# A chunked scan before two feed-forward blocks: how the first four chunks get their decay rows, and when

## The chip, the cores and the metric

The kernel runs on one core of one Trainium2 chip. The metric is the device time of one execution in microseconds, and the median of three runs is what counts. The core has five engines that run beside each other, each through its own list of instructions in order: PE (TensorE, matrix products), DVE (VectorE), ACT (ScalarE), POOL (GpSimd) and SP (SyncE, which here only issues transfers). Sixteen DMA engines carry the transfers, and an engine that has a transfer instruction in its list starts it and goes on.

## What is computed

A state-space scan over 4 batches, 8 heads, 768 steps, then a feed-forward block with an ELU, then a bilinear one. Cut to what matters here:

```python
def _attn_ref(x, a, B, C):                # x: 4 x 8 x 768 x 32, state width N = 16
    log_a = np.log(np.clip(a, 1e-06, 1.0))
    for c in range(nc):
        cum = np.cumsum(log_a[:, :, sl], axis=-1)
        L = np.exp(cum[..., :, None] - cum[..., None, :]) * causal
        M = np.einsum('bhin,bhjn->bhij', Cc, Bc) * L
        y[:, :, sl] = M @ xc + (Cc @ state) * np.exp(cum)[..., None]
        state = decay_full * state + (Bc * decay_from_j).T @ xc
...
h = x @ w_in                              # 3072 x 256 @ 256 x 2048
g = np.where(h > 0, h, np.exp(np.minimum(h, 0)) - 1)
x = g @ w_out                             # 2048 x 256
out = (((x @ w1) * (x @ w2)) @ w3) @ w_out2
```

`L` needs nothing but products of consecutive values of `a`. The kernel makes it by running products, without a logarithm.

## The kernel before

The scan works on 24 chunks of 128 steps, each as two halves of 64, with all eight heads at once. Four chunks make one tile of 512 tokens, and there are six tiles. All later products take every operand as a high and a low part in fp32r and use three matmuls for each (`mm3`). So each piece of a weight (512 KB) goes through three stages: a load (line 136), bit work on DVE and ACT (lines 146 to 148) and a split into the two parts (lines 103 and 104). The pieces of the first block are `wi0` to `wi7` (`raw_wi` in the profile) and `wo0` to `wo7` (`raw_wo`).

One chunk `k` of the first tile goes through four steps:

- `at_prep`: DVE makes `L` by one scan along the rows (line 334) from values of `a` that lie alike on all partitions of a half. POOL then makes `bd`, B times the decay to the chunk's end (line 340).
- `at_cb`: PE makes the products of C and B (`cb`, line 351), and DVE multiplies them into `L` (line 359).
- the state step: POOL makes `cd` from C and the running products `pr` (line 373), PE makes `u` (line 387), and DVE brings the state `st` forward (lines 396 and 399). `pr` is made once for four chunks by `at_decay` (lines 261 to 303).
- `at_y`: PE makes `y` from `L` and from the state (lines 416 and 422), ACT copies out its high part `xTh` (line 431), and DVE its low part `xTl` (line 432).

For chunks 4 and later the values of `a`, with 0 put at each half's first place, are written once to DRAM (`a_cut`), and each half of an `L` tile is filled from there by a transfer that gives the same 2 KB row to 64 partitions (line 312). For chunks 0 to 3 the values come another way. `at_first` loads all of `a` (`a_f`), bounds it, cuts it and splits it for PE. `at_wide` then has PE spread the rows over the partitions by products with a 0/1 matrix (`sel`; the result is `aw`, line 321).

The order of the first tile is a table, `ORDER`. A number is a step, 4k plus 0 for `at_prep`, 1 for `at_cb`, 2 for the state step and 3 for `at_y`. A pair is a weight piece and the stage to bring it to, `"pr"` is `at_decay(0)`, `"aw"` the second spreading product, and `"h"` the products of the first feed-forward unit for half of its tokens. After the table come the units of the feed-forward blocks, with the scan of later tiles laid between them. PSUM rooms for `cb`, `u`, `y` and `h` come from one pool of three that go round, so a `y` that isn't copied out holds back the third room request after it.

Every transfer reports its end on one of eight counters (`DMAHW0` to `DMAHW7`), handed out in turn as the transfers are scheduled, whatever engine issues them. Before a counter is used again, the issuing engine waits, in its own list, until the transfer that had it before has landed. Before the change only SP issues transfers.

Of the kernel before, what the change touches and what calls it, by code (L numbers as in the profile page):

```python
# [7 lines left out]
F32 = mybir.dt.float32  # L8
F32R = mybir.dt.float32r
# [4 lines left out]
NB, NH, S, D, N = 4, 8, 768, 32, 16  # L14
Q = 128
SUB = 2
R = Q // SUB
CPB = S // Q
NCHUNK = NB * CPB
TT = 512  # L20
NTILE = NB * S // TT
CPT = TT // Q
# [11 lines left out]
PACE, LATE, END, FIRST = 1.5, 12.0, 7.0, 8.0  # L34
SPILL, BACK = 3, 8

ORDER = [0, 4, 1, "pr", 2, "aw", (0, 2), 5, 3, 6, (0, 3), 8, 7, 9, (1, 2), 10, 12, 11, 13, (1, 3), 14, "h", 15, (2, 2), (3, 2)]


XCOLS = (("x", DM), ("bn", NH * N), ("bt", 2 * R), ("cz", 2 * 2 * R), ("cp", SUB * 2 * R))  # L40
# [3 lines left out]
def kernel(  # L44
# [20 lines left out]
    nc = tc.nc  # L65
    P = 128

    const = ctx.enter_context(tc.tile_pool(name="const", bufs=1))
    wts = ctx.enter_context(tc.tile_pool(name="wts", bufs=1))
    act = ctx.enter_context(tc.tile_pool(name="act", bufs=2))  # L70
    att = ctx.enter_context(tc.tile_pool(name="att", bufs=2))
    ps_w = ctx.enter_context(tc.tile_pool(name="ps_w", bufs=3, space=bass.MemoryType.PSUM))
    ps_a = ctx.enter_context(tc.tile_pool(name="ps_a", bufs=1, space=bass.MemoryType.PSUM))

    V, A, G, T = nc.vector, nc.scalar, nc.gpsimd, nc.tensor


    eye2 = const.tile([P, SUB, R], F32, name="eye2")
    eye = const.tile([P, NH, R], F32, name="eye")
    side = const.tile([P, 2], F32, name="side")  # L80
    sel = const.tile([SUB * CPT, CPT, SUB, R], F32R, name="sel")
    begun = const.tile([P, CPT * SUB, R], F32, name="begun")

    def constants():

        V.memset(side, 0.0)
        A.activation(side, side, AF.Exp)

        G.memset(eye2, 1.0)
        G.affine_select(out=eye2, in_=eye2, compare_op=ALU.is_equal, fill=0.0, base=0,  # L90
                        pattern=[[-R, SUB], [-1, R]], channel_multiplier=1)
        n = SUB * CPT
        A.copy(sel, eye2[:n, 0, :n].rearrange("p (k s o) -> p k s o", k=CPT, o=1).to_broadcast([n, CPT, SUB, R]))
        V.tensor_tensor(out=eye2[:, 0], in0=eye2[:, 0], in1=eye2[:, 1], op=ALU.add)
        V.tensor_copy(eye, eye2[:, 0:1].to_broadcast([P, NH, R]))
        G.memset(begun, 0.0)
# [69 lines left out]
    a = slice(None)  # L166
# [87 lines left out]
    ck = [{} for _ in range(NCHUNK)]  # L254
    xT = {}
    state = {}
    a_cut = tc.dram_tile([NCHUNK * SUB, NH, R], F32, name="a_cut")
    cut = []

    def clip(eng, out, v):  # L260
        return eng.tensor_scalar(out, v, 1e-6, 1.0, op0=ALU.max, op1=ALU.min)

    def at_first():


        t = act.tile([P, 2, NH, R], F32, tag="p", name="a_f")[:SUB * NCHUNK, 0]
        nc.sync.dma_start(t, a_s)
        clip(V, t, t)
        V.memset(t[:, :, 0:1], 0.0)
        n = SUB * CPT  # L270
        hl = act.tile([P, 2, NH, R], F32R, tag="p", name="a_hl")[:n]
        split(hl[:, 0], hl[:, 1], t[:n], V)
        cut.extend([hl, t])

    def at_load(k):
        c = ck[k]
        all_ = att.tile([P, XC], F32, tag="xbc", name=f"xbc{k}", bufs=4)
# [12 lines left out]

    def at_pr(t):

        pr[t] = att.tile([P, CPT * SUB, R], F32, tag="pr", name=f"pr{t}", bufs=2)
        nc.sync.dma_start(pr[t].rearrange("p k i -> p (k i)"),
                          a_h[t].rearrange("h (o s) -> h o s", o=1).to_broadcast([NH, N, TT]))

    def at_decay(t):

        v = pr[t]
        pace(clip(V, v, v))  # L300
        V.tensor_copy(begun[:, :, 0:1], v[:, :, 0:1])
        V.memset(v[:, :, 0:1], 0.0)  # L302
        V.tensor_tensor_scan(out=v.rearrange("p k i -> p (k i)"), data0=v.rearrange("p k i -> p (k i)"),
                             data1=begun.rearrange("p k i -> p (k i)"), initial=0.0, op0=ALU.mult, op1=ALU.add)

    def at_l(k):
        c = ck[k]
        c["L"] = att.tile([P, NH, R], F32, tag="L", name=f"L{k}", bufs=3)
        if k >= CPT:

            for s in range(SUB):
                nc.sync.dma_start(c["L"][R * s:R * s + R].rearrange("p h s -> p (h s)"),
                                  a_cut[SUB * k + s:SUB * k + s + 1].rearrange("s h i -> s (h i)").to_broadcast([R, NH * R]))

    def at_wide(k):


        wide = ps_a.tile([P, 2, TT], F32, tag="acc", name=f"aw{k}") if k else banks(f"aw{k}")
        for j in range(2):
            for p in range(2):  # L320
                mm = T.matmul(wide[:, j], sel[:, k + j].rearrange("r s i -> r (s i)"),
                              cut[0][:, p].rearrange("r h i -> r (h i)"), start=p == 0, stop=p == 1)
                if j == p == 0:
                    tc.keep_in_program_order(mm)
            ck[k + j]["a"] = wide[:, j]

    def at_prep(k):

        c = ck[k]
        L = c["L"]  # L330
        flat = wide = L.rearrange("p h s -> p (h s)")
        if k < CPT:
            wide = c["a"]
        made = V.tensor_tensor_scan(out=flat, data0=wide, data1=eye.rearrange("p h s -> p (h s)"), initial=0.0,
                                    op0=ALU.mult, op1=ALU.add)
        pace(made)
        if k < CPT:
            last_mm[:] = [made.ins]
        c["bd"] = att.tile([P, NH, N], F32, tag="bd", name=f"bd{k}")
        G.tensor_tensor(out=c["bd"], in0=c["bn"], in1=L[:, :, R - 1:R].to_broadcast([P, NH, N]), op=ALU.mult)  # L340

    def cb_products(k, cb):

        c = ck[k]
        for g in range(2):
            for r in range(4):
                s, b = divmod(r, 2)
                rows = slice(32 * r, 32 * r + 32)  # L350
                mm = T.matmul(cb[R * s:R * s + R, b, 2 * R * g:2 * R * g + 2 * R], c["bt"][rows, g], c["cz"][rows, g],  # L351
                              start=True, stop=True, skip_group_check=True)
                if k == g == r == 0:
                    tc.keep_in_program_order(mm)
        return mm

    def decayed(k, cb):
# [233 lines left out]
    made = 0  # L591
# [56 lines left out]
    queue, due = [], []  # L648
# [49 lines left out]

    at_first()
    constants()  # L700
    at_load(0)
    at_pr(0)
    queue[0].advance(1)
    for k in range(1, CPT):
        at_load(k)
    for p in queue[1:3]:
        p.advance(1)
    nc.sync.dma_start(a_cut, cut[1])
    for p in queue[3:8]:
        p.advance(1)  # L710
    for k in range(CPT):
        at_l(k)
    at_wide(0)
    for p in queue[:first_n]:
        p.lo = V

    for j in ORDER:
        if j == "pr":
            at_decay(0)
        elif j == "aw":  # L720
            at_wide(2)
# [82 lines left out]
```

## Time and profile before

| | us |
|---|---|
| median of 3 runs | 576.53 (576.19 to 577.77) |
| profiled execution, device time | 577.51 |
| its span in the trace | 575.8 |
| PE busy in the span | 553.8 (96%) |
| DVE busy | 338.4 (59%) |
| ACT busy | 273.3 (47%) |
| POOL busy | 85.8 (15%) |

The busy times are shares of the whole span, in which the stages differ much. The first 28 us hold the scan of the first tile, and up to about 60 us weight pieces are being made on DVE and ACT beside the first feed-forward units. After that PE is nearly always at work. In the rows below, us count from the span's start, and "issue" rows of SP show when SP issued a transfer, not when it landed.

### The profile page before, as it was taken

How to read it: one execution, taken by the hardware profiler on the slowest of the kernel's cores; microseconds unless marked ns; L12 is line 12 of the kernel's file. 1: busy time of each engine (PE TensorE's matmuls, PEld its weight loads, DVE VectorE, ACT ScalarE, POOL GpSimd, SP SyncE). 2: the span in 40 equal slices, each digit the busy share in tenths (PEclk: the TensorE clock that was granted, in tenths of full speed). 3: DMA queues.
4: the chain of work that ended last, by engine and by line, in shares of the span. 5: the costliest groups of instructions: out<-in, count | busy, mean ns of one | idle time of the engine just before them, and what ended most of it. 6: DMA issues, size and time to landing. Idle time of an engine off the chain costs nothing.

```text
span 575.8 us, 10500 instructions
## 1 busy us (share of the span) xinstructions
PE 553.8 (96%) x4436; PEld 442.1 (77%) x4436; DVE 338.4 (59%) x483; ACT 273.3 (47%) x375; POOL 85.8 (15%) x91
## 2 busy tenths in 40 slices
PE   5998998999999999999999999999999999999996
PEld 3675786788888888878787878877878868888784
DVE  6599999784976764756524444253766353244332
ACT  2296669445575565873214222222644452364222
POOL 2201324232204231550000000000111000000000
PEclk9998999899999999999999999999999999999999
DMA  8977453644333412550000421021000000000000
GB/s 289 332 235 235 135 163 121 201 155 150 114 139 131 135 70 102 190 146 1 0 1 37 157 83 56 0 94 56 37 19 2 1 2 0 1 37 0 1 1 36
DMA packets 27167, 52.78 MB, mean 92 GB/s; under 512 B 2192, under 2 KB 10384, under 8 KB 27120
## 3 DMA queue, kind: packets, MB, share of 16 engines
q1 hardware_dynamic: 27120, 52.11, 28.0%
q8 instruction: 35, 0.57, 0.5%
q14 instruction: 12, 0.10, 0.1%
HBM read 45.71 MB, written 6.39 MB: 90 GB/s over the span
## 4 chain that ended last, share of the span: by engine, by line
PE 79%; DVE 11%; issue 3%; ACT 3%; DMA 2%; POOL 1%; SPq 0%; DVEq 0%; POOLq 0%
PE ab L241 8%; PE ab L240 8%; PE ab L242 7%; PE acc_b L241 6%; PE acc_b L240 6%; PE acc_b L242 6%; PE h L240 6%; PE h L242 5%; PE h L241 5%; PE acc_d L241 4%; PE acc_d L240 4%; PE acc_d L242 4%; DMA raw_wa<-in_w 2%; PE s L351 2%; DVE e L523 1%
## 5 line engine op out<-in xcount | busy, mean ns | idle before, releaser
L523 DVE SCALAR_TENSOR_TENSOR e<-e,h 128x1024 f32<-128x1024 f32 x48 | 58.3, 1215 | 40.6 <-ACT e L522 40.5
L104 DVE TENSOR_TENSOR g<-e,g 128x1024 fp32r<-128x1024 f32 x48 | 60.2, 1255 | 34.9 <-ACT g L103 34.6
L240 PE MATMUL h<-xTh,w_in_lo 128*128 128x512 f32 (+1 forms) x196 | 77.5, 396 | 2.2 <-DVE pr L302 0.6
L240 PE MATMUL acc_b<-g,w_out_lo 128*128 128x512 f32 x192 | 77.1, 402 | 2.2 <-DVE x2l L104 1.9
L241 PE MATMUL acc_b<-g,w_out_hi 128*128 128x512 f32 x192 | 76.5, 399 | 1.0 <-DVE g L104 0.9
L103 ACT CAST g<-e 128x1024 fp32r<-128x1024 f32 x48 | 50.5, 1053 | 54.8 <-PE acc_b L242 30.2
L242 PE MATMUL acc_b<-g,w_out_hi 128*128 128x512 f32 x192 | 76.4, 398 | 0.0
L241 PE MATMUL h<-xTl,w_in_hi 128*128 128x512 f32 (+1 forms) x196 | 76.2, 389 | 0.0
L242 PE MATMUL h<-xTh,w_in_hi 128*128 128x512 f32 (+1 forms) x196 | 76.2, 389 | 0.0
L240 PE MATMUL ab<-x2h,w 128*128 128x512 f32 x192 | 74.2, 392 | 1.7 <-ACT x2h L103 1.4
L241 PE MATMUL ab<-x2l,w 128*128 128x512 f32 x192 | 75.0, 391 | 0.1
L242 PE MATMUL ab<-x2h,w 128*128 128x512 f32 x192 | 74.7, 389 | 0.0
L520 ACT ACTIVATE e<-h 128x1024 f32<-128x1024 f32 x48 | 49.3, 1028 | 42.5 <-PE h L242 39.9
L568 DVE TENSOR_TENSOR pa<-pa,ab 128x512 f32<-128x512 f32 x48 | 32.6, 685 | 59.1 <-ACT pa L567 59.1
L567 ACT COPY pa<-ab 128x512 f32<-128x512 f32 x48 | 27.9, 588 | 74.2 <-PE ab L242 73.6
L104 DVE TENSOR_TENSOR p<-pa,p 128x512 fp32r<-128x512 f32 x48 | 32.9, 690 | 40.4 <-ACT p L103 40.2
L103 ACT CAST p<-pa 128x512 fp32r<-128x512 f32 x48 | 29.8, 621 | 48.0 <-PE acc_d L242 28.6
L522 ACT ACTIVATE e<-e 128x1024 f32<-128x1024 f32 x48 | 51.2, 1066 | 0.9
L240 PEld LDWEIGHTS h<-xTh,w_in_lo 128*128 128x128 f32 x196 | 37.2, 190 | 11.3 <-DVE pr L302 0.9
L240 PEld LDWEIGHTS acc_b<-g,w_out_lo 128*128 128x128 f32 x192 | 36.6, 191 | 10.8 <-DVE x2l L104 2.1
L240 PEld LDWEIGHTS ab<-x2h,w 128*128 128x128 f32 x192 | 35.9, 188 | 10.6 <-ACT x2h L103 2.3
L241 PEld LDWEIGHTS acc_b<-g,w_out_hi 128*128 128x128 f32 x192 | 36.7, 191 | 9.1 <-DVE g L104 1.7
(106 smaller groups left out, 891.9 us busy)
## 6 DMA issues: line engine op xcount, KB each, us to landing
xbc<-in_xc SPq DMA_DIRECT2D x24, 512.0 KB, 6.0
raw_wc<-in_w3t SPq DMA_DIRECT2D x16, 512.0 KB, 3.4
L<-a_cut SPq DMA_DIRECT2D x40, 128.0 KB, 4.5
raw_wi<-in_w_in SPq DMA_DIRECT2D x8, 512.0 KB, 8.3
raw_wo<-in_w_out SPq DMA_DIRECT2D x8, 512.0 KB, 4.6
out_t<-o SPq DMA_DIRECT2D x12, 256.0 KB, 2.0
raw_wq<-in_wo SPq DMA_DIRECT2D x4, 512.0 KB, 3.4
raw_wb<-in_w SPq DMA_DIRECT2D x4, 512.0 KB, 6.1
```

The costliest lines, as they stand in the source:

```text
L103: A.copy(hi, raw)
L104: return lo_eng.tensor_tensor(out=lo, in0=raw, in1=hi.bitcast(F32), op=ALU.subtract)
L240: last_mm[:] = [T.matmul(out, wlo, xhi, start=first, stop=False, **kw).ins]
L241: T.matmul(out, whi, xlo, start=False, stop=False, **kw)
L242: T.matmul(out, whi, xhi, start=False, stop=last, **kw)
L351: mm = T.matmul(cb[R * s:R * s + R, b, 2 * R * g:2 * R * g + 2 * R], c["bt"][rows, g], c["cz"][rows, g], start=True, stop=True, skip_group ...
L520: A.activation(e, h, AF.Exp)
L522: A.activation(e, e, AF.Relu, scale=-1.0, bias=1.0)
L523: V.scalar_tensor_tensor(out=e, in0=e, scalar=-1.0, in1=h, op0=ALU.mult, op1=ALU.max)
L567: A.copy(e, h[:, 0])
L568: V.tensor_tensor(out=e, in0=e, in1=h[:, 1], op=ALU.mult)
```

## The change

- Chunks 0 and 1 (`DIRECT = 2`) get their `L` tiles by transfers straight from the input `a_s`, and DVE bounds and cuts each tile itself (`bounded`). Chunks 2 and 3 get theirs from `a_cut`, as later chunks do. The `L` tiles of the first tile are four rooms instead of three.
- The spreading products, `sel` and the split of `a` are gone.
- For chunks 0 to 3 the `L` transfers, and the one that writes `a_cut`, are issued by ACT instead of SP.
- `pr` is made behind the first `L`.
- The data of all four chunks are issued ahead of all weight pieces (before, the first piece stood ahead of chunk 1's data).
- The table has another order: the making of piece `wi0` stands later against the chunks, as does that of `wi1`.

```diff
-ORDER = [0, 4, 1, "pr", 2, "aw", (0, 2), 5, 3, 6, (0, 3), 8, 7, 9, (1, 2), 10, 12, 11, 13, (1, 3), 14, "h", 15, (2, 2), (3, 2)]
+DIRECT = 2
+
+ORDER = [0, "pr", 1, 2, 4, 5, 3, 6, (0, 2), 8, 7, 9, (0, 3), 10, 12, 11, 13, (1, 2), 14, "h", (1, 3), 15, (2, 2), (3, 2)]
...
         t = act.tile([P, 2, NH, R], F32, tag="p", name="a_f")[:SUB * NCHUNK, 0]
         nc.sync.dma_start(t, a_s)
-        clip(V, t, t)
-        V.memset(t[:, :, 0:1], 0.0)
-        n = SUB * CPT
-        hl = act.tile([P, 2, NH, R], F32R, tag="p", name="a_hl")[:n]
-        split(hl[:, 0], hl[:, 1], t[:n], V)
-        cut.extend([hl, t])
+        cut.append(t)
+
+    def bounded(v):
+        clip(V, v, v)
+        V.memset(v[:, :, 0:1], 0.0)
...
     def at_l(k):
+
         c = ck[k]
-        c["L"] = att.tile([P, NH, R], F32, tag="L", name=f"L{k}", bufs=3)
-        if k >= CPT:
-
-            for s in range(SUB):
-                nc.sync.dma_start(c["L"][R * s:R * s + R].rearrange("p h s -> p (h s)"),
-                                  a_cut[SUB * k + s:SUB * k + s + 1].rearrange("s h i -> s (h i)").to_broadcast([R, NH * R]))
...
+        c["L"] = att.tile([P, NH, R], F32, tag="L", name=f"L{k}", bufs=4)
+
+        for s in range(SUB):
+            (A if k < CPT else nc.sync).dma_start(
+                c["L"][R * s:R * s + R].rearrange("p h s -> p (h s)"),
+                (a_s if k < DIRECT else a_cut)[SUB * k + s:SUB * k + s + 1].rearrange("s h i -> s (h i)").to_broadcast([R, NH * R]))
...
-        flat = wide = L.rearrange("p h s -> p (h s)")
-        if k < CPT:
-            wide = c["a"]
-        made = V.tensor_tensor_scan(out=flat, data0=wide, data1=eye.rearrange("p h s -> p (h s)"), initial=0.0,
+        flat = L.rearrange("p h s -> p (h s)")
+        if k < DIRECT:
+            bounded(L)
+        made = V.tensor_tensor_scan(out=flat, data0=flat, data1=eye.rearrange("p h s -> p (h s)"), initial=0.0,
                                     op0=ALU.mult, op1=ALU.add)
...
+    for k in range(DIRECT):
+        at_l(k)
     at_first()
     constants()
     at_load(0)
     at_pr(0)
-    queue[0].advance(1)
     for k in range(1, CPT):
         at_load(k)
-    for p in queue[1:3]:
+    bounded(cut[0])
+    A.dma_start(a_cut, cut[0])
+    for k in range(DIRECT, CPT):
+        at_l(k)
+    for p in queue[:8]:
         p.advance(1)
-    nc.sync.dma_start(a_cut, cut[1])
-    for p in queue[3:8]:
-        p.advance(1)
-    for k in range(CPT):
-        at_l(k)
-    at_wide(0)
```

What this does to the lists of the engines shows best on ACT. Its list before, from the copy for the spreading products on; the number after a name's letters is the chunk or the piece (`raw_wi0`, `y1`), the last number only tells buffers apart, and the brackets name what the instruction waits for:

```order
L103 CAST a_hl_93<-a_f_89 8x512 [waits DVE_49]
L147 ACTIVATE raw_wi0_108<-raw_wi0_108 128x512 [waits DMAHW3_49]
L103 CAST w_in_hi_78<-raw_wi0_108 128x2x256 [waits DVE_49]
L431 CAST xTh0_218<-y0_193 128x2x2x64 [waits PE_49]
L431 CAST xTh0_218<-y1_244 128x2x2x64 [waits PE_49]
L147 ACTIVATE raw_wi1_116<-raw_wi1_116 128x512 [waits DMAHW7_49]
L103 CAST w_in_hi_78<-raw_wi1_116 128x2x256 [waits DVE_49]
L431 CAST xTh0_218<-y2_310 128x2x2x64 [waits PE_49]
L431 CAST xTh0_218<-y3_387 128x2x2x64 [waits PE_49]
```

And ACT's list after the change, from its fifth instruction on:

```order
L692 DMA a_cut_85<-a_f_94 48x512 [waits DMAHW1_49,DVE_49]
L309 DMA L2_116<-a_cut_85 64x512 [waits DMAHW1_49]
L309 DMA L2_116<-a_cut_85 64x512 [waits DMAHW3_49]
L309 DMA L3_119<-a_cut_85 64x512 [waits DMAHW5_49]
L309 DMA L3_119<-a_cut_85 64x512 [waits DMAHW7_49]
L415 CAST xTh0_212<-y0_187 128x2x2x64 [waits PE_49]
L146 ACTIVATE raw_wi0_122<-raw_wi0_122 128x512
L102 CAST w_in_hi_77<-raw_wi0_122 128x2x256 [waits DVE_49]
L415 CAST xTh0_212<-y1_237 128x2x2x64 [waits PE_49]
L415 CAST xTh0_212<-y2_304 128x2x2x64 [waits PE_49]
L146 ACTIVATE raw_wi1_124<-raw_wi1_124 128x512 [waits DMAHW4_49]
```

Five transfers, four of them with a wait on a landing counter, now stand on ACT ahead of the first copy out of a `y`. SP's list in the same program, from chunk 1's data on:

```order
L275 DMA xbc1_107<-in_xc 128x1024
L275 DMA xbc2_109<-in_xc 128x1024 [waits DMAHW0_49]
L275 DMA xbc3_111<-in_xc 128x1024 [waits DMAHW2_49]
L135 DMA raw_wi0_122<-in_w_in 128x2x512 [waits DMAHW3_49]
L135 DMA raw_wi1_124<-in_w_in 128x2x512 [waits DMAHW4_49]
L135 DMA raw_wi2_126<-in_w_in 128x2x512 [waits DMAHW5_49]
L135 DMA raw_wo0_128<-in_w_out 128x2x512 [waits DMAHW6_49]
L135 DMA raw_wi3_130<-in_w_in 128x2x512 [waits DMAHW7_49]
L135 DMA raw_wo1_132<-in_w_out 128x2x512 [waits DMAHW0_49]
```

Of the five weight pieces up to `wi3`, `wi0`, `wi2` and `wi3` stand on the counters 3, 5 and 7, which ACT's last three transfers wait for too. DVE's list after the change, from the end of chunk 1 to the scan of chunk 2 (line 320, 334 before):

```order
L380 SCALAR_TENSOR_TENSOR st1_1_229<-st1_0_227,pr0_105,u1_218 128x64 [waits DVE_49]
L416 TENSOR_TENSOR xTl0_213<-y0_187,xTh0_212 128x2x2x64 [waits Activation_49]
L145 TENSOR_SCALAR raw_wi0_122<-raw_wi0_122 128x512 [waits DMAHW3_49]
L147 SCALAR_TENSOR_TENSOR raw_wi0_122<-raw_wi0_122 128x512 [waits DVE_49,Activation_49]
L103 TENSOR_TENSOR w_in_lo_78<-raw_wi0_122,w_in_hi_77 128x2x256 [waits Activation_49]
L416 TENSOR_TENSOR xTl0_213<-y1_237,xTh0_212 128x2x2x64 [waits Activation_49]
L320 SCALAR_TENSOR_TENSOR L2_116<-L2_116,eye_74 128x512 [waits DMAHW3_49,DMAHW1_49]
```

The making of `wi0` and the low parts of two `y` stand between chunk 1 and chunk 2 there; before, `wi0` was made beside chunk 0.

## Rows read from the trace of the kernel before

**Rows 1.** Busy time by stage: us, each engine (instructions), granted clock, DMA share, GB/s.
```profile
0.00:30.00 30.00, 22.77 (x403) 15.77 (x404) 18.68 (x41) 8.92 (x17) 7.03 (x15) 1.00 0.95 308
30.00:60.00 30.00, 26.28 (x211) 19.49 (x210) 30.00 (x46) 23.79 (x32) 5.15 (x5) 0.94 0.73 222
60.00:576.00 516.00, 504.74 (x3825) 406.84 (x3824) 289.76 (x398) 240.57 (x328) 73.60 (x72) 0.99 0.22 71
```

**Rows 2.** What DVE waited for, 24 to 62 us: total, times, longest.
```profile
DVE xTl L432 <- ACT xTh L431: 3.7, 1, 3.7
```

**Rows 3.** What PE waited for, 28 to 62 us, first and last of five.
```profile
PE s L387 <- POOL bd L340: 2.5, 2, 1.9
...
PE acc_b L240 <- ACT g L103: 0.3, 1, 0.3
```

**Rows 4.** ACT in order of time, 2 to 29 us: start, duration, what [idle before <-releaser].
```profile
8.69 0.67 ACT L147 ACTIVATE raw_wi<-raw_wi 128x512 f32<-128x512 f32 x1 [4.56 <-DMA raw_wi<-in_w_in]
14.33 0.37 ACT L431 CAST xTh<-y 128x256 fp32r<-128x256 f32 x1 [2.52 <-PE y L422]
27.37 0.37 ACT L431 CAST xTh<-y 128x256 fp32r<-128x256 f32 x1 [5.02 <-PE y L422]
```

**Rows 5.** SP's issues in order of time, 0 to 27 us.
```profile
0.80 0.40 SPq L267 DMA_DIRECT2D a_f<-in_a_s  x1
8.69 0.37 SPq L136 DMA_DIRECT2D raw_wi<-in_w_in  x1
19.15 5.69 SPq L312 DMA_DIRECT2D L<-a_cut  x4
```

**Rows 6.** Transfers issued at 8.7, 19.2 and 53.3 us: count, KB each, us to landing.
```profile
raw_wi<-in_w_in SPq DMA_DIRECT2D x1, 512.0 KB, 10.4
L<-a_cut SPq DMA_DIRECT2D x1, 128.0 KB, 12.0
L<-a_cut SPq DMA_DIRECT2D x2, 128.0 KB, 2.9
```

**Rows 7.** Busy time in short stretches, columns as in rows 1; the last two are DMA.
```profile
2.00:3.00 1.00, 0.00 (x0) 0.00 (x0) 0.10 (x1) 0.79 (x3) 0.00 (x0) 1.00 0.62 154
4.00:5.00 1.00, 0.82 (x2) 0.39 (x2) 0.68 (x1) 0.13 (x1) 0.00 (x0) 1.00 0.78 207
10.00:19.00 9.00, 7.32 (x178) 4.45 (x177) 6.78 (x16) 1.99 (x4) 3.36 (x5) 1.00 1.04 397
21.00:24.00 3.00, 2.91 (x51) 2.12 (x51) 2.44 (x7) 1.02 (x2) 1.62 (x2) 1.00 1.05 234
27.00:33.00 6.00, 5.15 (x49) 4.03 (x38) 5.22 (x11) 5.63 (x10) 0.00 (x0) 1.00 1.02 249
```

**Rows 8.** DVE in order of time, 0 to 28 us.
```profile
2.90 0.42 DVE L261 TENSOR_SCALAR a_f<-a_f 48x512 f32<-48x512 f32 x1 [1.97 <-DMA a_f<-in_a_s]
6.58 2.34 DVE L334 TENSOR_TENSOR_SCAN L<-aw,eye 128x512 f32<-128x512 f32 x2 [1.74 <-PE aw L321]
11.17 1.22 DVE L303 TENSOR_TENSOR_SCAN pr<-pr,begun 128x512 f32<-128x512 f32 x1
14.73 0.42 DVE L432 TENSOR_TENSOR xTl<-y,xTh 128x256 fp32r<-128x256 f32 x1 [0.96 <-ACT xTh L431]
15.07 1.21 DVE L334 TENSOR_TENSOR_SCAN L<-aw,eye 128x512 f32<-128x512 f32 x1
21.94 0.69 DVE L104 TENSOR_TENSOR w_in_lo<-raw_wi,w_in_hi 128x512 fp32r<-128x512 f32 x1 [0.53 <-ACT w_in_hi L103]
22.55 0.42 DVE L432 TENSOR_TENSOR xTl<-y,xTh 128x256 fp32r<-128x256 f32 x1
```

**Rows 9.** PE in order of time, 18 to 28 us.
```profile
23.02 0.58 PE L240 MATMUL h<-xTh,w_in_lo 128*128 128x256 f32 x1
25.88 0.68 PE L416 MATMUL y<-L,xbc 64*32 64x64 f32 x32
```

**Rows 10.** POOL in order of time, 6 to 28 us.
```profile
16.36 0.41 POOL L340 TENSOR_TENSOR bd<-xbc,L 128x128 f32<-128x128 f32 x1 [1.20 <-DVE L L334]
```

More of the change, by code (lines that the diff above doesn't have):

```diff
@@ L80 @@
     side = const.tile([P, 2], F32, name="side")
-    sel = const.tile([SUB * CPT, CPT, SUB, R], F32R, name="sel")
     begun = const.tile([P, CPT * SUB, R], F32, name="begun")
@@ L91, in constants @@
                         pattern=[[-R, SUB], [-1, R]], channel_multiplier=1)
-        n = SUB * CPT
-        A.copy(sel, eye2[:n, 0, :n].rearrange("p (k s o) -> p k s o", k=CPT, o=1).to_broadcast([n, CPT, SUB, R]))
         V.tensor_tensor(out=eye2[:, 0], in0=eye2[:, 0], in1=eye2[:, 1], op=ALU.add)
@@ L267, in at_first @@
         nc.sync.dma_start(t, a_s)
-        clip(V, t, t)
-        V.memset(t[:, :, 0:1], 0.0)
-        n = SUB * CPT
-        hl = act.tile([P, 2, NH, R], F32R, tag="p", name="a_hl")[:n]
-        split(hl[:, 0], hl[:, 1], t[:n], V)
-        cut.extend([hl, t])
+        cut.append(t)
+    def bounded(v):
+        clip(V, v, v)
+        V.memset(v[:, :, 0:1], 0.0)
     def at_load(k):
@@ L307, in at_l @@
         c = ck[k]
-        c["L"] = att.tile([P, NH, R], F32, tag="L", name=f"L{k}", bufs=3)
-        if k >= CPT:
-            for s in range(SUB):
-                nc.sync.dma_start(c["L"][R * s:R * s + R].rearrange("p h s -> p (h s)"),
-                                  a_cut[SUB * k + s:SUB * k + s + 1].rearrange("s h i -> s (h i)").to_broadcast([R, NH * R]))
[L315 to L325, printed above, removed]
+        c["L"] = att.tile([P, NH, R], F32, tag="L", name=f"L{k}", bufs=4)
[3 more added lines that the diff above has]
+                (a_s if k < DIRECT else a_cut)[SUB * k + s:SUB * k + s + 1].rearrange("s h i -> s (h i)").to_broadcast([R, NH * R]))
     def at_prep(k):
@@ L352, in cb_products @@
                               start=True, stop=True, skip_group_check=True)
-                if k == g == r == 0:
-                    tc.keep_in_program_order(mm)
         return mm
@@ L719 @@
             at_decay(0)
-        elif j == "aw":
-            at_wide(2)
         elif j == "h":
```

## Prediction

> **What bounds the kernel now.** I read the busy times by stage first. After 60 us PE is busy 505 of 516 us, so whatever the start loses or gains stays to the end [rows 1]. From 30 to 60 us DVE is busy 30 of 30 us and PE is not: there the kernel lives on DVE, which makes weight pieces [rows 1]. Next I read DVE's waits. From 24 to 62 us it waits once, 3.7 us, for ACT's copy of chunk 3's y [rows 2]. So DVE's backlog begins when that copy is there, at 27.37 us [rows 4], and no transfer is late in the backlog. A shift of that moment shifts DVE's backlog, then PE's, then the end, one for one. Everything the change touches lies before it. The question is when `xTh` of y3 can start.
>
> Before, `xTh` of y0 starts at 14.33 and `xTh` of y3 at 27.37, 13.04 us apart [rows 4]. Those are the two marks I follow.
>
> **Removed.** The spreading products and the split of `a` stand ahead of the first scan: DVE reads `a_f` at 2.90 and starts the scans of L0 and L1 only at 6.58, after waiting for `aw`; the two end at 8.92 [rows 8]. Now L0 comes by transfer. The nearest row is `a_f`, issued at 0.80 and read at 2.90, 2.1 us [rows 5, 8]. L0's second half is ACT's second issue, about 1.2 us into the span, and lands at about 3.5; bounding (0.42, by the row of `a_f`) and one scan (1.2) end at about 5.3. The first `L` is some 2.4 us earlier, for it was done at 7.7, half way through the pair. `pr` follows it and not the making of `wi0`; its scan stood at 11.17 [rows 8] and can be 2 us earlier.
>
> **Added on DVE.** Two bounding steps of 0.42 and two small clearings, 1 us together. They lie in the time that chunk 0 gained. Had that no cover, it would cost 1 us of the 2.4.
>
> **Moved, and the term that decides.** Eight transfers of half an `L` each and the one that writes `a_cut` are now in ACT's list, ahead of its first copy of a y. Before, ACT issued nothing, so what such a wait does is read from SP. SP issues `wi3` at 8.69, and ACT begins on `wi0` at the same 8.69, released by the landing of `wi0` [rows 4, 5]: the piece that held the counter had to land first, and SP stood still meanwhile. That hurt nobody, since SP only issues. On ACT it holds all that follows.
>
> What ACT waits for follows from the counters. There are eight, handed out in turn: L0's first half has 0, `a_f` 1, chunk 0's data 2, L0's second half 3, `pr` 4, L1's halves 5 and 7, chunk 1's data 6; then chunk 2's data 0, `a_cut` 1, chunk 3's data 2, and `wi0`, `wi1`, `wi2`, `wo0`, `wi3` take 3 to 7. So L2's second half waits for `wi0`, L3's first half for `wi2`, its second half for **wi3**. That these are the users is seen in ACT's list: the bit work on `wi0` there has no wait left, while that on `wi1` has one. Therefore the first `xTh` cannot start before `wi3` has landed, the last of 11 transfers on SP. Behind it on ACT stand the making of `wi0` and every later copy. DVE's low part of y0 waits for it, and behind that in DVE's list the making of `wi0` and the scans of chunks 2 and 3; PE waits for y0's room to make `cb` of chunk 2.
>
> **When does wi3 land?** Before, it was issued at 8.69 and took 10.4 us, to 19.1 [rows 5, 6]. Ahead of it went `a_f`, four chunks' data, `pr`, `wi0` to `wi2`, `wo0` and `a_cut`. The same go ahead of it now, and seven of the eight halves of L besides, 7 x 131 = 917 kB. The DMA engines are full: share 1.04 at 397 GB/s from 10 to 19 us [rows 7].
> - At least: 917 kB at 397 GB/s are 2.3 us, less the room that ACT's early issues can fill, 0.38 + 0.22 us that the engines were idle in the stretches 2 to 3 and 4 to 5 [rows 7]. That is 1.7, `wi3` at 20.8.
> - At most: where these one-row-to-64 transfers run, the rate falls. From 27 to 33 us, in which the four of chunks 4 and 5 fall (issued from 19.15 on, the first landing 12.0 us later), 249 GB/s are moved at share 1.02; 234 from 21 to 24, where the next `pr` of like kind stands in the queue [rows 5 to 7]. Six us at 249 GB/s are 1494 kB, which need 3.8 us at 397: 2.2 us lost for four, 0.56 each. With its own bytes (0.33) one half costs 0.89 us, seven 6.2: `wi3` at 25.3.
>
> I take 5.2, near the upper end, because the slow stretch is the same kind of transfer: `wi3` at 24.3. With 0.4 us for ACT's last issue (SP's took 0.40 [rows 5]) `xTh` of y0 starts at 24.7 instead of 14.33: **10.4 us late**. What chunks 0 and 1 gained is hidden in this: their last products are done by about 15, nine us before ACT is free.
>
> The row shows full engines with SP's queue alone. The Trainium skill, "DMA: Bandwidth & Descriptors", section "Issuing engines are not separate DMA queues", says that transfers from any issuer run on the same 16 engines and that several issuers save issue time only. By that the 917 kB push `wi3` back as above; if ACT's queue ran beside SP's instead, `wi3` would stay at 19.1. The latter is a rival below.
>
> **From y0 to y3 after the hold.** Up to the scan of L2 it took 0.74 us (14.33 to 15.07); now the making of `wi0` with ACT's part and two low parts stand there, about 3.4 (0.40 to the first low part, three steps of 0.3 to 0.7, ACT's 0.65 between, a second low part) [rows 4, 8]. From that scan to the low part of y2 it took 7.5 us (15.07 to 22.55) with the making of `wi1` in between; that now stands behind, so I count 1.3 to `bd`, 0.4 for it, and 2.7 for `u`, a state step, `y` and its copy: 4.4 [rows 8, 10]. From there to `xTh` of y3, 4.8 as before: `h` at 23.02, then y at 25.88, then the copy [rows 4, 9]. Sum 12.6 against 13.04, so 0.4 us comes back. This stretch has `wi0` to `wi3` at hand, so no weight is late in it.
>
> **Sum.** 10.4 - 0.4 = **10.0 us later**. On the profiled execution that is 577.5 + 10.0 = 587.5; it lies 1.0 above the median of the runs, so for the median 576.5 + 10.0 = **586.5**. The products taken from PE (eight) lie where PE waits and give nothing. The ends of `wi3` give 6.5 and 11.0: 583 to 587.5.
>
> **Rivals.**
> - *L3 lands late.* With SP's queue full a half took 12.0 us to land, in a quiet stretch 2.9 [rows 6]. L3's second half is issued at 24.3; the scan of L3 is due some 6.4 us later, so at 2.9 it is hidden, at 10 it costs about 3.5: 590. The Trainium skill, the same page, section "Queues, rings and completion order", says SP and ACT have rings of their own on each engine, which serves them in turn; by that the half passes SP's backlog and the sum stays 586.5. No row shows ACT's queue. Chance 0.12.
> - *ACT's transfers run beside SP's.* Then `wi3` lands at 19.1 and the shift is 19.1 + 0.4 - 14.3 - 0.4 = 4.8: 581.3. Against it: share 1.04 [rows 7]. 0.10.
> - *Part is absorbed.* PE's five groups of waits from 28 to 62 us are 4.3 together, from 2.5 for POOL's `bd` down to 0.3 [rows 3], and the units there stand in a slightly other order. If all of it went, 582.2. Against it: DVE is full [rows 1]. 0.10.
> - *Faster: ACT is not held when it matters.* If `wi3` landed before y0 is done, the time removed ahead of L0 would come through, 2.4 us: 574.1. It decides at `wi3` = 14.3 us. For it: the first L is earlier for sure. Against it: some 6.1 MB lie ahead of and in `wi3`, and at 397 GB/s from 2 us on that is 17 us at the least. It needs the counters to be other than I read them. 0.05.
>
> **How the numbers follow.** Forecast 0.63, then 0.12, 0.10, 0.10, 0.05. The time is the forecast's, 586.5. The range takes in the ends of `wi3` and the first three rivals, with a us on either side for the new order of units: 580.5 to 591. A measurement of this kernel tells 0.3% (1.7 us) from no change. Faster by more: 0.05, the last rival. Within: 0.04, cases where little hold and much absorption meet. Slower: 0.91.
>
> **What would show it.** After the change ACT should stand idle ahead of its first `xTh` until about 24 us, released by the landing of a `raw_wi`, while `cb` of chunk 2 follows the low part of y0. The rate should fall to about 250 GB/s wherever the halves of L run. `xTh` of y3 should start at about 37.4, and DVE should be full from then on with the same waits as before. I am wrong if `xTh` of y0 starts near 12, or if `xTh` of y3 is 10 us late and the end is not.

## The result, and the profile after

The kernel after takes 585.31 us (median of 4 runs, 583.76 to 586.24) against 576.36 for the kernel before (4 runs): a ratio of 1.0147, with a 95% interval of 1.0126 to 1.0168, or 8.95 us. The profiled execution took 584.75 us with a span of 583.0, 7.2 us more than that of before.

Busy time by stage, kernel after (columns as in [rows 1]):

```profile
0.00:30.00 30.00, 8.68 (x260) 5.91 (x264) 13.77 (x31) 3.34 (x6) 4.55 (x13) 1.00 0.95 285
30.00:60.00 30.00, 26.98 (x248) 21.34 (x240) 26.59 (x44) 21.59 (x31) 3.69 (x5) 0.94 0.77 237
60.00:583.00 523.00, 510.81 (x3932) 412.04 (x3932) 300.36 (x413) 246.89 (x336) 75.89 (x73) 0.99 0.23 73
```

In the first 30 us PE's work fell from 22.8 to 8.7 us, DVE's from 18.7 to 13.8 and ACT's from 8.9 to 3.3. Of the 14.1 us that PE has less, 4.4 are the eight spreading products (2.36 and 2.07 us before); the rest is for the most part work that has been put off. Behind 60 us PE is busy nearly all of the time in both kernels, so the delay stays.

The reason stands in ACT's list. Its waits from 0 to 40 us, kernel after (total, times, longest):

```profile
ACT xTh L415 <- DMA L<-a_cut: 17.8, 1, 17.8
```

And ACT in order of time, with the four copies `xTh` of y0 to y3, which answer to [rows 4]:

```profile
12.13 10.62 ACTq L309 DMA_DIRECT2D L<-a_cut  x4
22.80 0.37 ACT L415 CAST xTh<-y 128x256 fp32r<-128x256 f32 x1 [17.81 <-DMA L<-a_cut]
...
25.35 0.36 ACT L415 CAST xTh<-y 128x256 fp32r<-128x256 f32 x1
30.66 0.37 ACT L415 CAST xTh<-y 128x256 fp32r<-128x256 f32 x1 [4.95 <-PE y L406]
...
36.87 0.37 ACT L415 CAST xTh<-y 128x256 fp32r<-128x256 f32 x1 [2.56 <-PE y L406]
```

PE's last products of y0, kernel after:

```profile
13.29 0.65 PE L406 MATMUL y<-cd,st 32*32 32x64 f32 x16
```

The reader is to see three things. ACT computes nothing for 17.8 us, and half of that holds something up: y0 is ready for its copy at 13.94, 8.9 us before the copy starts. What stands ahead of its first copy is a row of `ACTq`, four issues that take 10.6 us because each waits for a landing. And the copy of y3, the mark that I followed, starts at 36.87 instead of 27.37: 9.5 us late, against 8.95 in the medians.

SP's issue of `wi3`, and the landing times of transfers issued at 12.0, 15.6, 18.9, 22.3 and 2.7 us (they answer to [rows 5, 6]):

```profile
12.01 0.47 SPq L135 DMA_DIRECT2D raw_wi<-in_w_in  x1
```

```profile
raw_wi<-in_w_in SPq DMA_DIRECT2D x1, 512.0 KB, 10.3
L<-a_cut ACTq DMA_DIRECT2D x1, 128.0 KB, 7.0
L<-a_cut ACTq DMA_DIRECT2D x1, 128.0 KB, 6.5
L<-a_cut ACTq DMA_DIRECT2D x1, 128.0 KB, 7.5
L<-in_a_s ACTq DMA_DIRECT2D x1, 128.0 KB, 8.9
```

`wi3` lands at 12.0 + 10.3 = 22.3 us, ACT's last issue follows at 22.3, and the copy of y0 at 22.8. The chain is the one that the prediction named.

DVE in order of time, kernel after (it answers to [rows 8]):

```profile
6.60 0.43 DVE L260 TENSOR_SCALAR L<-L 128x512 f32<-128x512 f32 x1 [2.77 <-DMA L<-in_a_s]
...
7.20 1.23 DVE L320 TENSOR_TENSOR_SCAN L<-L,eye 128x512 f32<-128x512 f32 x1
...
23.21 0.42 DVE L416 TENSOR_TENSOR xTl<-y,xTh 128x256 fp32r<-128x256 f32 x1 [7.53 <-ACT xTh L415]
...
26.42 1.22 DVE L320 TENSOR_TENSOR_SCAN L<-L,eye 128x512 f32<-128x512 f32 x1
...
29.87 1.22 DVE L320 TENSOR_TENSOR_SCAN L<-L,eye 128x512 f32<-128x512 f32 x1 [0.51 <-DMA L<-a_cut]
31.07 0.42 DVE L416 TENSOR_TENSOR xTl<-y,xTh 128x256 fp32r<-128x256 f32 x1
```

Behind chunk 1's state step DVE stands still for 7.5 us until ACT's copy, then does in one go what it did piece by piece before. From the copy of y3 on its waits are as few as in [rows 2]; 37 to 75 us, kernel after:

```profile
DVE xTl L416 <- ACT xTh L415: 2.2, 1, 2.2
DVE e L507 <- ACT e L506: 0.3, 1, 0.3
```

### The profile page after: what moved, and what is told of

It is laid out like the page before. It is cut to its first block, busy times and chain, and to the rows that moved or that the text cites. A ratio compares the mean times of both kernels' runs of the same rounds, so it can differ in the third digit from the quotient of the medians.

```text
span 583.0 us, 10493 instructions
## 1 busy us (share of the span) xinstructions
PE 546.5 (94%) x4428; PEld 439.3 (75%) x4428; DVE 340.7 (58%) x486; ACT 271.8 (47%) x373; POOL 84.1 (14%) x91
## 3 DMA queue, kind: packets, MB, share of 16 engines
q10 hardware_dynamic: 704, 1.15, 0.8%
## 4 chain that ended last, share of the span: by engine, by line
PE 76%; DVE 8%; DMA 6%; ACT 4%; issue 3%; POOL 1%; SPq 0%; DVEq 0%; POOLq 0%; ACTq 0%
PE ab L240 7%; PE ab L241 7%; PE ab L239 7%; PE acc_b L239 6%; PE acc_b L240 6%; PE acc_b L241 6%; PE h L239 5%; PE h L241 5%; PE h L240 5%; PE acc_d L240 4%; PE acc_d L239 4%; PE acc_d L241 4%; DMA raw_wa<-in_w 2%; DMA raw_wo<-in_w_out 2%; DVE g L103 2%
## 5 line engine op out<-in xcount | busy, mean ns | idle before, releaser
L240 PE MATMUL acc_b<-g,w_out_hi 128*128 128x512 f32 x192 | 75.5, 393 | 1.6 <-DVE g L103 1.6
L241 PE MATMUL acc_b<-g,w_out_hi 128*128 128x512 f32 x192 | 75.3, 392 | 0.0
L239 PEld LDWEIGHTS ab<-x2h,w 128*128 128x128 f32 x192 | 35.9, 188 | 10.7 <-ACT x2h L102 2.3
```

Source lines behind the costliest of these rows:

```text
L239: last_mm[:] = [T.matmul(out, wlo, xhi, start=first, stop=False, **kw).ins]
L240: T.matmul(out, whi, xlo, start=False, stop=False, **kw)
L241: T.matmul(out, whi, xhi, start=False, stop=last, **kw)
```

## The experiments

The theory at first was that the hold in ACT's list makes the loss and the new order costs nothing. After the first four runs it became: the hold costs about 6 of the 9 us, and the transfers ahead of the first weight piece cost the rest. Throughout, whatever moves the copy of y3 was to move the end by as much. The rivals were that the transfers as such, or the order, or the lost products make the difference, with the hold only a symptom. The runs go from the hold to the rest.

**The hold alone, put into the kernel before.** One small write to DRAM, issued by ACT, reads the landed piece `wi3`, or in a second kernel `wi4`, so that ACT waits for that piece ahead of its first copy (the copies of y0 and y1 are kept behind it in the list). Nothing else is changed, and no transfer of `L` is added.

```diff
+        if j == 5:
+            held.append(A.dma_start(scr, queue[4].raw[0:1, 0:TT // 2].rearrange("p a b -> p (a b)")))
```

> The same write, made from wi3, which lands at about 19.1 us before. Theory: xTh of y0 starts at about 19.5 instead of 14.3, 5.2 later; y3's copy is 4 to 5.5 us later and the median 580 to 582.5, between before and the run with wi4. Rival: within 1.7 us of before.

> The kernel before with one thing added: ACT issues a 2 KB write to DRAM that reads the landed wi4, in its list ahead of the copies of y0 and y1. Nothing else of the scan changes. wi4 lands at about 22.3 us, so xTh of y0 should start at about 22.8, as in the changed kernel. Theory (the hold on ACT is the cost): y3's copy moves by 7.5 to 9 us and the median is 583 to 586. Rival (the cost is the slower landing and the other order, ACT could wait for nothing): within 1.7 us of before, 575 to 578.

ACT in order of time, first with `wi3`, then with `wi4`:

```profile
19.30 0.65 ACT L434 CAST xTh<-y 128x256 fp32r<-128x256 f32 x2 [7.54 <-DMA raw_wi<-in_w_in]
...
31.12 0.37 ACT L434 CAST xTh<-y 128x256 fp32r<-128x256 f32 x1 [5.27 <-PE y L425]
```

```profile
24.25 0.65 ACT L434 CAST xTh<-y 128x256 fp32r<-128x256 f32 x2 [12.52 <-DMA raw_wi<-in_w_in]
...
35.63 0.37 ACT L434 CAST xTh<-y 128x256 fp32r<-128x256 f32 x1 [4.83 <-PE y L425]
```

The first copy comes 5.0 us late by the one and 9.9 by the other, that of y3 3.75 and 8.26. The times are 581.81 us (1.0089, 1.0066 to 1.0111) and 582.96 (1.0105, 1.0077 to 1.0133), against 576.52. The first time is as expected, with the copy of y3 just short of its 4 to 5.5; the second is just below its range of 583 to 586. A hold on ACT alone makes a loss of this size. That the longer one makes it larger by 1.15 us is not clear of the noise: the two intervals overlap. The second came to 6.4 us for 8.3 of shift; but the shift is read from the profiled execution, which at 585.30 us was the slowest of the four.

**The hold taken away.** The change as it is, but all four chunks get `L` straight from the input, so that ACT has no transfer behind a weight piece:

```diff
-DIRECT = 2
+DIRECT = 4
```

> The changed kernel with all four chunks loaded straight from the input (DIRECT = 4): ACT's eight halves then wait only for early landings and none for a weight piece. Theory (hold): xTh of y0 starts when y0 is done, at 14 to 16 us; y3's copy at 27 to 30; the median 575.5 to 579.5. Rival (the bytes and slow transfers of L are the cost): these stay, 1 MB of them, so 583 or more.

ACT in order of time:

```profile
14.30 0.37 ACT L415 CAST xTh<-y 128x256 fp32r<-128x256 f32 x1
18.69 0.66 ACT L146 ACTIVATE raw_wi<-raw_wi 128x512 f32<-128x512 f32 x1 [4.02 <-DMA raw_wi<-in_w_in]
...
20.96 0.37 ACT L415 CAST xTh<-y 128x256 fp32r<-128x256 f32 x1
...
30.97 0.37 ACT L415 CAST xTh<-y 128x256 fp32r<-128x256 f32 x1 [2.05 <-PE y L406]
```

579.44 us (8 runs), 1.0053 (1.0037 to 1.007). The copy of y0 is back at 14.30, as in [rows 4], with the same four chunks' data ahead and as many halves of `L`. So 5.9 of the loss of 8.8 (585.31 - 576.52) went with the hold, near the 6.4 that the longer hold had made alone. Of the rest, 2.9 us, the rows show the place: the making of `wi0` waits 4.0 us for the piece, which now lands at 18.7 instead of 8.7, and the copy of y1 stands behind it, 3.4 us late. The copy of y3 was expected at 27 to 30 and is at 30.97; the time is inside its range.

**The first piece ahead again.** The same kernel with `wi0` loaded ahead of the data of chunks 1 to 3, as before the change:

```diff
     at_pr(0)
+    queue[0].advance(1)
     for k in range(1, CPT):
         at_load(k)
```

> The run with all four L loaded straight from a (no a_cut, no hold on ACT), now also with wi0 issued ahead of the data of chunks 1 to 3, as in the kernel before. Theory, that the 2.9 us left in that run are wi0's late landing (18.7 us), which holds ACT and DVE ahead of the copy of y1: here wi0 lands at 9 to 13 us, the copy of y1 starts at 17.5 to 18.5 instead of 20.96, that of y3 at 27.4 to 28.5 instead of 30.97, and the time is 576.5 to 578. Rival, that the 2.9 us are the slow transfers of eight halves as such, whichever comes first: another transfer (data of a chunk, a later weight) then holds a copy as long, y3 stays at 30 or later and the time at 579 or more.

580.11 us, 1.0059 (1.0037 to 1.0081): no gain, and the copy of y3 at 30.72 instead of 30.97. My theory on the rest was wrong, and its rival right. PE in order of time shows what is late in the place of `wi0`:

```profile
14.58 1.13 PE L337 MATMUL cb<-xbc 32*64 32x128 f32 x16 [4.85 <-DMA xbc<-in_xc]
```

Chunk 1's data come 4.85 us late for PE, and the copy of y0 falls from 14.30 to 16.97. Whichever transfer goes behind the halves of `L`, one is late: the rest of the loss is most likely their room in the DMA engines, and the order in front only chooses who waits. DVE's bounding of the tiles, 0.42 us for each, is in both kernels too and was not tried by itself.

**The order alone.** The kernel before, with its spreading products, in the new order and with the four chunks' data ahead of the weights.

```diff
-ORDER = [0, 4, 1, "pr", 2, "aw", (0, 2), 5, 3, 6, (0, 3), 8, 7, 9, (1, 2), 10, 12, 11, 13, (1, 3), 14, "h", 15, (2, 2), (3, 2)]
+ORDER = [0, "pr", 1, 2, 4, "aw", 5, 3, 6, (0, 2), 8, 7, 9, (0, 3), 10, 12, 11, 13, (1, 2), 14, "h", (1, 3), 15, (2, 2), (3, 2)]
...
-    queue[0].advance(1)
```

> The kernel before, spreading products kept, with the order of the changed one alone: the data of four chunks ahead of wi0, pr behind the first L, wi0 and wi1 made where the change makes them. Theory (hold is all): the order is worth little, y3's copy moves by less than 1.5 us, 575 to 578. Rival (the order costs the most): y3's copy is 4 us late or more and the median at or above 580.

576.44 us (10 runs), 0.9997 (0.9983 to 1.0011). The copy of y3 is at 26.99, 0.4 us earlier. The order and the place of the data cost nothing by themselves; that leaves the halves of `L`, with what DVE does to them, for the rest.

**What makes the halves dear?** The halves of L0 and L1 read 64 distinct rows each, in place of one row 64 times:

```diff
-                (a_s if k < DIRECT else a_cut)[SUB * k + s:SUB * k + s + 1].rearrange("s h i -> s (h i)").to_broadcast([R, NH * R]))
+                (a_cut[SUB * k + s:SUB * k + s + 1].rearrange("s h i -> s (h i)").to_broadcast([R, NH * R]) if k >= DIRECT
+                 else xc[20 + k, R * s:R * s + R, 0:NH * R]))
```

> The changed kernel, but the four halves of L0 and L1 are loaded from 64 distinct rows each of the packed input in place of one row of a read 64 times; the same bytes, queues and counters. (So the decay factors of chunks 0 and 1 are other numbers than the reference's; no step is left out.) Theory, that reading one row into 64 partitions is what lowers the rate: between 5 and 9 us the engines move over 300 GB/s at full share instead of 248 to 281, L0 is there at about 5.5 us instead of 6.6, wi3 lands at 20.5 to 21.5 instead of 22.3, the first copy of y0 starts as much earlier than 22.80, and the time is 583 to 584.5. Rival, that any transfer into 64 partitions of 2 KB each costs the same and only its bytes count: the rate, L0, wi3 and the time stay as in the changed kernel, 584.5 to 586.

Two short stretches, first of the kernel after, then of this one (columns as in [rows 7]):

```profile
5.00:9.00 4.00, 1.15 (x20) 0.75 (x20) 1.83 (x4) 0.00 (x0) 0.41 (x1) 1.00 1.06 261
9.00:12.00 3.00, 0.82 (x24) 0.58 (x28) 2.76 (x7) 0.00 (x0) 0.52 (x1) 1.00 1.02 330
```

```profile
5.00:9.00 4.00, 1.37 (x32) 0.96 (x32) 1.72 (x3) 0.00 (x0) 0.41 (x1) 1.00 0.94 243
```

Per unit of share that is 246 and 259 GB/s. The copy of y0 starts at 22.35 instead of 22.80, L0 is there at 6.38 instead of 6.60, and the time is 586.30 us (1.016, 1.0129 to 1.0192), not lower. So the one row read 64 times isn't what makes these transfers slow; the forecast's term went by the right rows with a wrong word for their cause.

A second kernel puts 1 MB each of four kinds of transfer behind the last output of the kernel before, where nothing else runs.

```diff
+        for b, j, rows in half:
+            load(b[rows], a_s[4 * j:4 * j + 4:2].rearrange("(o k) h i -> o k (h i)", o=1).to_broadcast([R, 2, TT]))
+        for b, j, rows in half:
+            load(b[rows], xc[20 + 2 * j:22 + 2 * j, rows, 0:TT].rearrange("k r w -> r k w"))
...
+        for b, j, rows in half[:2]:
+            load(b.rearrange("p k w -> p (k w)"), xc[20 + j])
```

> The kernel before with 24 transfers of 128 to 512 KB added behind its last output, when the DMA engines are otherwise idle: four megabytes, twice, each first in 2 KB rows into 64 partitions with one row repeated 64 times (the kind of the L halves), then 2 KB rows into 64 partitions from distinct rows, then 2 KB rows into 128 partitions, then 4 KB rows into 128 partitions (the kind of the chunk data). Its time is longer by these transfers, and only the bytes per busy time of the DMA engines in each are read. Theory, that 2 KB rows cost more for a byte than 4 KB rows, whatever repeats: about 250 GB/s per unit of share for the first three, about 390 for the last. Rival 1, that 64 partitions cost: 250 for the first two, 390 for the last two. Rival 2, that the repeated row costs: 250 for the first only. Rival 3, that none of it costs by itself and the low rate comes from two queues running at once: 390 for all four.

By the order and the sizes of the packets in the trace, the second round has the repeated rows from 585.6 to 590.0 us, the distinct rows of 2 KB to 594.7, the 2 KB rows into 128 partitions to 599.1 and the 4 KB rows to 603.2; in the first round distinct rows ran from 570.1 to 573.9 (its repeated rows were issued earlier, from 502.9 us). Five stretches, two of repeated rows, two of distinct rows (the second round's, then the first's), one of 4 KB rows (the last two columns are DMA share and GB/s):

```profile
586.00:587.00 1.00, 0.00 (x0) 0.00 (x0) 0.00 (x0) 0.00 (x0) 0.00 (x0) 0.50 0.83 246
589.00:590.00 1.00, 0.00 (x0) 0.00 (x0) 0.00 (x0) 0.00 (x0) 0.00 (x0) 0.50 1.05 248
...
591.00:592.00 1.00, 0.00 (x0) 0.00 (x0) 0.00 (x0) 0.00 (x0) 0.00 (x0) 0.50 0.99 225
572.00:573.00 1.00, 0.00 (x0) 0.00 (x0) 0.00 (x0) 0.00 (x0) 0.00 (x0) 1.00 0.93 264
...
600.00:601.00 1.00, 0.00 (x0) 0.00 (x0) 0.00 (x0) 0.00 (x0) 0.00 (x0) 0.50 0.84 307
```

By the unit of share these are 296 and 236, 227 and 284, and 365 GB/s. None of the four outcomes that I had written down is there: repeated rows and distinct rows each ran at a higher and at a lower rate, so the kind of transfer doesn't set it. Nor does the size of a row. In the 397 GB/s of [rows 7], 10 to 19 us, 3.0 of 3.6 MB went in packets of 2 KB. What makes the rate fall to about 250 stays open.

**Another issuer.** The change with all its halves and the writing of `a_cut` issued by SP:

```diff
-            (A if k < CPT else nc.sync).dma_start(
+            nc.sync.dma_start(
...
-    A.dma_start(a_cut, cut[0])
+    nc.sync.dma_start(a_cut, cut[0])
```

> The changed kernel with all its L halves and the writing of a_cut issued by SP instead of ACT, in the same places of the program. Theory, that ACT's hold cost some 6 of the 9 us: ACT stands still no more for its own list and copies y0 at 13.5 to 16; but the halves of L2 and L3 now stand in SP's list behind the weights and in its full queue, so that L2 is there at 24 to 28, DVE and PE wait for it, the copy of y3 starts at 33 to 38 and the time is 582 to 587: a hold of another kind in the place of the first. Rival, that what hurts is only which engine issues: the copy of y3 at 27.5 to 30.5, the time 577 to 580.

DVE and ACT in order of time:

```profile
30.20 1.23 DVE L320 TENSOR_TENSOR_SCAN L<-L,eye 128x512 f32<-128x512 f32 x1 [10.53 <-DMA L<-a_cut]
```

```profile
15.97 0.37 ACT L415 CAST xTh<-y 128x256 fp32r<-128x256 f32 x1 [13.68 <-PE y L406]
...
40.36 0.37 ACT L415 CAST xTh<-y 128x256 fp32r<-128x256 f32 x1 [1.52 <-PE y L406]
```

589.83 us, 1.0244 (1.021 to 1.0279), and above the 582 to 587 that I expected. ACT is free for y0 at 15.97, as the theory has it, but L2 is there only at 30.2 (24 to 28 expected), since its halves stand behind the weights in SP's list and take 12.1 and 11.2 us in SP's full queue. The wait changed its engine and grew. The copy of y3 is 13.0 us late, and the end 13.5.

**Forward instead of back.** If the copy of y3 sets the end, the kernel before can gain by it. In its table `"h"`, twelve products of the first feed-forward unit, stands ahead of the step that makes y3.

```diff
-ORDER = [0, 4, 1, "pr", 2, "aw", (0, 2), 5, 3, 6, (0, 3), 8, 7, 9, (1, 2), 10, 12, 11, 13, (1, 3), 14, "h", 15, (2, 2), (3, 2)]
+ORDER = [0, 4, 1, "pr", 2, "aw", (0, 2), 5, 3, 6, (0, 3), 8, 7, 9, (1, 2), 10, 12, 11, 13, (1, 3), 14, 15, "h", (2, 2), (3, 2)]
```

> The kernel before with one edit: the first half of the weight products (h) stands behind the place of y3's products and copy instead of ahead of them. Theory, that DVE's backlog begins at the copy of y3 and that a shift of this copy goes to the end one for one, backwards too: the copy starts at 25.2 to 25.9 instead of 27.37, and the time is 574 to 575.2. Rival, that the backlog only begins early with nothing ready to feed PE, so that h, now later, is missed at the end of it: the copy is as early, the time stays at 576 to 577 or is longer.

> The kernel before with the changed kernel's order of the first scan (which alone made no difference) and h behind y3. By the theory that y3's copy sets the end: copy of y3 at 25 to 25.7, time 573.8 to 575. By the rival (h is missed later): 576 to 577.5. If the order of the scan matters beside that of h, it differs from the run with h alone by over 0.5 us.

With `"h"` behind, alone: 575.61 us (12 runs), 0.9985 (0.9971 to 0.9999), the copy of y3 at 27.01, 0.36 earlier and not 1.5 to 2.2; both miss what I expected. PE in order of time shows why:

```profile
24.32 0.42 PE L422 MATMUL y<-cd,st 32*32 32x64 f32 x4
25.91 1.06 PE L422 MATMUL y<-cd,st 32*32 32x64 f32 x28 [1.17 <-issue]
```

The last products of y3 stop after 4 of 32 for 1.17 us, with no wait that the profile names. With the new order besides, 574.62 us (12 runs, against 576.49), 0.9976 (0.9959 to 0.9993), inside the 573.8 to 575 expected, the copy of y3 at 26.18, half a us behind its 25 to 25.7; here the stop is 0.78. Without the stops the two copies would have come at about 25.8 and 25.4, both as expected (estimates: 27.01 - 1.17 and 26.18 - 0.78). This is the fastest kernel here by its median, 1.9 us below the kernel before and 10.7 below the change; the 1.0 us to `"h"` behind alone is not clear of the noise.

## Why the prediction was right

The forecast was 586.5 us, and 585.31 was measured. Its reason was that ACT stands in its own list until `wi3` has landed, and this is shown: by the row of 17.8 us, by the hold put in alone and by the hold taken away. But two of its terms were off, by 1.9 us down and 1.5 up, and nearly cancelled each other; that the number came within 1.2 us is in part luck.

| step | predicted | measured |
|---|---|---|
| `wi3` landed | 24.3 (20.8 to 25.3) | 22.3 |
| from there to the copy of y0 | 0.4 | 0.5 |
| copy of y0, late by | 10.4 | 8.5 (22.80 - 14.33) |
| copy of y0 to copy of y3 | 12.6 | 14.07 |
| copy of y3, late by | 10.0 | 9.5 |
| end, late by | 10.0 | 8.95 (medians) |

- *The landing of `wi3`* was mis-sized by 2.0 us, most likely through the count. I took seven halves to be ahead of `wi3`, since seven are issued before it lands. But only the four of L0 and L1 are issued ahead of it, and L2's first half 0.1 us behind it, at 12.13. Two of the seven are held by landings themselves: L2's second half is issued at 15.6, when `wi0` is there, and lands at 22.6; L3's first is issued at 18.9, when `wi2` is there, and lands at 25.4. By the same price four halves give 3.0 us (4 x 0.89 - 0.6) and five 3.9; measured were 3.2 more than before. The price itself was tried by no run, and its reason, one row read 64 times, was wrong. All of the 3.2 had arisen by the issue: `wi3` was issued at 12.01 instead of 8.69, directly behind `wo0`, which had waited for chunk 1's data until 11.6, and then took 10.3 us as before (10.4). So the halves most likely pushed `wi3` back through SP's own waits on landings.
- *The stretch to y3* was 1.5 us longer than I had. Up to the scan of L2 it is 3.6 us (3.4 predicted), from there to the low part of y2 4.65 (4.4), where the 0.51 of waiting for L3's half lies. The rest, about 1.0, is behind y2, where I took over the 4.8 us of before and 5.8 were needed. There the last of y's 32 products starts 0.90 us after the others, again with no wait that the profile names. In the kernel with own rows, which has the same order, this stop is missing and the whole stretch is 13.07 (22.35 to 35.42). PE in order of time, kernel after:

```profile
34.64 0.45 PE L400 MATMUL y<-L,xbc 64*32 64x64 f32 x31
35.98 0.24 PE L400 MATMUL y<-L,xbc 64*32 64x64 f32 x1 [0.90 <-issue]
```

- *The first `L`* did not come early. I took 2.1 us for its landing by the row of `a_f`, and its last half took 5.1: L0 is there at 6.6, its scan ends at 8.4, and the first scan of before was done at 7.7. Nothing hung on it, because this was hidden in the hold. Without the hold it could have been the gain.
- *The markers*: ACT idle until about 24 and the copy of y3 at about 37.4 came at 22.8 and 36.9. The rate was about 250 GB/s only from 5 to 9 us, and 330 from 9 to 12. One marker was wrong. `cb` of chunk 2 does not follow the low part of y0: it ran at 16.84, before it (23.21). It is the third room request behind y0, which should have been held back by a y0 that isn't copied out; here it had a free room. What PE waits for is `bd`, 10.2 us: POOL makes it from L2, whose scan stands behind the low part of y0 in DVE's list. So the hold reached PE through DVE's list and not through y0's room. PE in order of time, kernel after:

```profile
16.84 1.13 PE L337 MATMUL cb<-xbc 32*64 32x128 f32 x16
28.18 0.47 PE L371 MATMUL u<-xbc,bd 64*32 64x64 f32 x16 [10.21 <-POOL bd L326]
```

- *The rivals.* That ACT's transfers run beside SP's at no cost (581.3) is refuted by `wi3`, 3.2 us later. That L3 lands late (590) cost 0.5 instead of 3.5: its half took 7.5 us on ACT's queue. The Trainium skill, "DMA: Bandwidth & Descriptors", section "Queues, rings and completion order", has each DMA engine serve in turn the rings that have work. The landings agree as far as they go: 6.5 to 7.5 us on ACT's queue beside a full SP queue, 12.1 and 11.2 for the same halves in SP's. The section "Issuing engines are not separate DMA queues" says that another issuer saves issue time only. Here the choice was worth more than that: with SP as issuer the kernel took 4.5 us longer than with ACT (589.83 against 585.31), since the issuer chooses the list and the queue in which a transfer stands.
- *The faster rival* needed the counters to be other than I had read them, and they were not.

**One for one** was the last step. The ten kernels that differ in the first tile, the copy of y3 by their profiled execution and the time by medians, each against the kernel before in the same series:

| kernel | y3 copy at | y3 shift | time shift |
|---|---|---|---|
| new order, `h` behind y3 | 26.18 | -1.2 | -1.9 |
| new order alone | 26.99 | -0.4 | -0.1 |
| `h` behind y3 | 27.01 | -0.4 | -0.9 |
| four direct, `wi0` ahead | 30.72 | +3.4 | +3.6 |
| four direct | 30.97 | +3.6 | +2.9 |
| hold for `wi3` | 31.12 | +3.8 | +5.3 |
| own rows | 35.42 | +8.1 | +9.8 |
| hold for `wi4` | 35.63 | +8.3 | +6.4 |
| the change | 36.87 | +9.5 | +9.0 |
| SP issues | 40.36 | +13.0 | +13.5 |

The order is nearly the same in both columns, and no pair differs by more than 1.9 us. Some scatter is to be expected, since the mark is read from one execution and the time is a median: the profiled execution of own rows was the fastest of its four (583.07 us), that of the hold for `wi4` the slowest (585.30). TensorE's clock moves the marks too. In the profiled execution of before it falls to 0.50, that is to 1.2 GHz, for 3.4 us at 102 us, behind a stretch in which PE was busy 2.11 of 4 us; PE is full there. Before and after, busy time by stretch:

```profile
98.00:102.00 4.00, 2.11 (x23) 1.34 (x23) 4.00 (x8) 3.88 (x6) 0.00 (x0) 1.00 0.72 260
102.00:105.40 3.40, 3.40 (x9) 2.62 (x10) 3.40 (x3) 0.91 (x1) 1.72 (x2) 0.50 0.84 265
```

```profile
102.00:105.40 3.40, 3.12 (x14) 2.52 (x15) 3.40 (x4) 3.32 (x5) 2.08 (x2) 1.00 0.00 0
```

SP's first two writes of `x_dramh`, before and then after, show what that is worth:

```profile
99.57 0.34 SPq L547 DMA_DIRECT2D x_dramh<-x2h  x1
156.51 1.37 SPq L547 DMA_DIRECT2D x_dramh<-x2h  x1
```

```profile
108.25 0.35 SPq L531 DMA_DIRECT2D x_dramh<-x2h  x1
163.59 1.23 SPq L531 DMA_DIRECT2D x_dramh<-x2h  x1
```

The shift is 8.7 us at the first write and 7.1 at the second, and between these marks only the profile of before has the low clock. But this does not explain why the profiled pair ends nearer (7.2) than the medians (8.95). Each of the two executions has two such falls, and the mean granted clock is 0.992 in both. The other fall of before is at 54.0 to 57.6 us (mean 0.53), those of after at 37 to 41 (0.58) and 60.0 to 67.0 (0.73 up to 63.4, 0.78 from there). How much of the scatter is the clock stays open.

## What to carry to other kernels

A transfer instruction is free for the engine that issues it only while it waits for nothing. Before giving transfers to an engine that computes, list what each of them waits for, a landing counter's earlier user included, and what stands behind it in that engine's list. And when several transfers share a full set of DMA engines, count as ahead only those that are issued by then, not all that will be: here that gives 3.0 us, against 3.2 measured and 5.2 forecast.

## What had not been expected of the hardware

- A 128 KB half of `L`, from the first microsecond on, took 5.1 to 8.9 us to land, where 96 KB of `a_f` issued at the same time were read 2.5 us after.
- The low rate, about 250 GB/s at full share, doesn't come from one row read 64 times (246 and 259 GB/s per unit of share with and without). In such a stretch packets of both sizes are slow. By the trace of before, the median packet of 2 KB took 84 ns from 10 to 19 us and 131 from 27 to 33, that of 4 KB 159 and 260. The cause is open.
- A run of like products on PE stops for 0.8 to 1.2 us in three of the kernels (0.90 in the change, 1.17 and 0.78 in the two with `"h"` behind), with no wait that the profile names. All three stop behind the 705th instruction of PE in the trace. In all three a 16 KB transfer on the DMA queue that the profile calls `instruction` had started 1.3 to 1.7 us ahead, at 33.18, 23.16 and 22.44 us, and the next product starts 1.3 to 1.5 us behind its end. In the kernel before and the seven others without such a stop this transfer had ended 1.5 us or more ahead of that place. So PE most likely waited for its own next instructions; no run was made to test it.
